# Attention over pooled slots and a top-128 MLP on one core: a planner's start order, GpSimd's drain and the final flag are changed

## Chip, core and metric

The kernel runs on one core of a Trainium2 chip. Its metric is the device time of one execution in microseconds (us). TensorE's weight loads (PEld) and matmuls (PE), VectorE (DVE), ScalarE (ACT), GpSimd (POOL) and SyncE (SP) each take their own instructions in the order in which they stand in the program; semaphores order them against each other.

## The reference, cut to what matters

```python
# q, k, v: 8 batches x 8 heads x 576 rows x 64;  phi: 8 x 8 x 576 x 32
a = softmax(phi, axis=2)                       # over the 576 rows
k_m = einsum('bhsm,bhsd->bhmd', a, k)          # 32 pooled keys per head
v_m = einsum('bhsm,bhsd->bhmd', a, v)          # 32 pooled values per head
x = softmax(q @ k_m.T / 8) @ v_m               # put together to 8 x 576 x 512
for b in range(8):
    top = the 128 rows of x[b] with the highest x[b] @ w_gate
    xe = x[b, top]
    out[b] = x[b]
    out[b, top] = xe + sigmoid(xe @ w_gate)[:, None] * (relu(xe @ w1) @ w2)   # 512 -> 1024 -> 512
```

## The kernel before

**The planner.** The program is written by Python generators (jobs), each of which issues a few instructions and then yields. `in_order_of_time` goes on with the job whose next step is due first by the costs of the class `Plan` (`plan.free` has the time at which each engine is free by these costs). These costs run when the program is built; on the chip only the order that came out of them is left. So a number in the planner moves instructions in all five queues, and changes none of them.

**Softmax of phi.** `softmax(b, chain)` makes an exact exponential of the 128 x 1152 tile of a batch: about twenty VectorE operations over 1152 elements (L381 to L448), half as many on ScalarE between them, and then normalises it (L454 to L476). Two chains take the even and the odd batches. `phi_loader` loads a batch's tile `ph` (L291).

**Keys.** `keys` transposes the finished softmax of a batch on TensorE (L580, four groups of three), splits it into two parts (`ahi` on ScalarE, `alo` on VectorE, L599), stores both to the DRAM tensor `aparts` (L605), and multiplies it with k (L622) to the pooled keys.

**Split of v.** `split_v` takes v in 32 pieces, four a batch, loads one (`vb`, L531, three buffers), rounds it on ScalarE (`vhi`, L548, two buffers), subtracts on VectorE (L550) and stores both parts to the DRAM tensor `vparts` from GpSimd's queue (L554). A piece isn't taken up before 8.0 + 6.5 us times its number by the planner's clock.

**Values.** The pooled values are summed in 116 chunks of 12 columns. Four batches can be under way, each in its 32 rows of the array and its own PSUM bank; `FIRST = [0, 8, 14, 20, 48, 56, 62, 68]` is the chunk with which a batch begins, and it lasts for 48. For every chunk `a_loader` reads `aparts` (L662), `v_loader` reads `vparts` (L686), `widener` spreads the weights over 128 columns in four operations on VectorE (L709) or ScalarE (L711), whichever the planner thinks is free, and `values` multiplies (L731).

**Attention and MLP.** When the pooled values of a batch are there, `centre` centres keys and values on VectorE (its last operation writes `vz`, L797) and TensorE transposes them (L801, L806); then come scores (L835), denominators (L896), products (L910), the gate's scores, the rank of each row (L1001) and the pick of 128 of them. `forward` gathers the picked rows (L1076), multiplies by w1 (L1112) and w2 (L1130), adds (`ye`, L1136) and scatters the rows to the output from GpSimd's queue (L1141). There are eight such scatters.

**The end.** A matmul with `ones` (L1183) sums the marks `good`, two small VectorE operations make the flag `any_bad` (L1185, L1189), every engine loads it into a register (L1190), and a branch (L1191) leaves out a slower general path when the flag is 0. Behind it the program ends with a barrier of all engines in which GpSimd drains (L1228).

## Time and profile before

| | us |
|---|---|
| median of 3 runs | 705.27 |
| lowest and highest | 701.38, 707.96 |
| profiled execution, its own time | 700.01 |
| its span, from the first to the last instruction | 698.3 |

The profiled execution lies below the lowest of the three runs, and its span leaves out 1.71 us of its time. The busy share of an engine says which engine could be the limit of a stage; idle time counts only where something is due that waits for it. The rows themselves stand in the section on rows below.

### The profile page before, as it was taken

How to read it: one execution, taken by the hardware profiler on the slowest of the kernel's cores; microseconds unless marked ns; L12 is line 12 of the kernel's file. 1: busy time of each engine (PE TensorE's matmuls, PEld its weight loads, DVE VectorE, ACT ScalarE, POOL GpSimd, SP SyncE). 2: the span in 40 equal slices, each digit the busy share in tenths (PEclk: the TensorE clock that was granted, in tenths of full speed). 3: DMA queues.
4: the chain of work that ended last, by engine and by line, in shares of the span. 5: the costliest groups of instructions: out<-in, count | busy, mean ns of one | idle time of the engine just before them, and what ended most of it. 6: DMA issues, size and time to landing. Idle time of an engine off the chain costs nothing. (4 is left out here: it accounts for less than half of the span.)

```text
span 698.3 us, 18467 instructions
## 1 busy us (share of the span) xinstructions
PE 469.8 (67%) x7130; PEld 386.9 (55%) x7130; DVE 550.3 (79%) x969; ACT 411.7 (59%) x739; POOL 298.8 (43%) x539
## 2 busy tenths in 40 slices
PE   0003285182651465767589879998999999999980
PEld 0002274172641454656567759878787788666750
DVE  4999999999799889897999969696245897978000
ACT  3457695687767798788665565646344655243110
POOL 6022651545525364674545445556455642112110
PEclk9999555555555789998999889999999999999995
DMA  8046775797958998789999766876648443212000
GB/s 215 3 138 194 247 216 174 227 292 254 285 190 263 316 292 241 228 269 255 329 315 340 227 210 212 261 234 209 186 145 231 131 149 127 76 54 69 31 15 20
DMA packets 69583, 137.37 MB, mean 197 GB/s; under 512 B 14832, under 2 KB 44528, under 8 KB 69488
## 3 DMA queue, kind: packets, MB, share of 16 engines
q0 software_dynamic: 25664, 84.45, 36.7%
q1 hardware_dynamic: 43824, 51.67, 26.6%
q8 instruction: 58, 0.95, 0.6%
q14 instruction: 37, 0.30, 0.2%
HBM read 96.21 MB, written 39.85 MB: 195 GB/s over the span
## 5 line engine op out<-in xcount | busy, mean ns | idle before, releaser
L731 PE MATMUL acc<-v_rows,a_rows 32*128 32x256 f32 x4608 | 223.9, 310 | 89.1 <-ACT a_rows L711 72.2
L731 PEld LDWEIGHTS acc<-v_rows,a_rows 32*128 32x128 f32 x4608 | 205.8, 213 | 112.3 <-ACT a_rows L711 70.9
L711 ACT ACTIVATE a_rows<-a_flat,block_of 128x384 fp32r<-128x384 f32 x306 | 164.8, 604 | 86.9 <-PE acc L731 39.9
L686 POOL DMA_DIRECT2D v_rows<-vparts x232 | 131.3, 579 | 114.4 <-PE acc L731 96.7
L709 DVE TENSOR_SCALAR a_rows<-a_flat,block_of 128x384 fp32r<-128x384 f32 x158 | 59.4, 417 | 51.2 <-PE acc L731 29.2
L662 POOL DMA_DIRECT2D a_flat<-aparts x116 | 65.2, 563 | 59.5 <-ACT a_rows L711 33.1
L580 PE MATMUL bank<-ident,ph 128*96 128x128 f32 x96 | 21.8, 373 | 77.2 <-DVE ph L476 77.2
L580 PEld LDWEIGHTS bank<-ident,ph 128*96 128x96 f32 x96 | 14.7, 192 | 82.2 <-issue 61.5
L554 POOL DMA_DIRECT2D vparts<-vb x32 | 19.5, 610 | 77.9 <-DVE vb L550 75.8
L1112 PE MATMUL bank<-xeT,w 128*128 128x128 f32 x352 | 44.3, 280 | 5.3 <-ACT xeT L1096 5.3
L1112 PEld LDWEIGHTS bank<-xeT,w 128*128 128x128 f32 x352 | 41.0, 192 | 7.8 <-ACT xeT L1096 6.5
L954 POOL DMA_DIRECT2D out<-xj x24 | 16.4, 682 | 56.5 <-DVE xj L950 23.3
L1001 DVE SCALAR_TENSOR_TENSOR marks<-row,tg,wide 128x576 bf16<-128x576 f32 x40 | 32.7, 818 | 8.5 <-ACT row L985 6.8
L997 ACT ACTIVATE marks<-row,tg 128x576 bf16<-128x576 f32 x40 | 31.1, 777 | 1.8
L1130 PE MATMUL bank<-w,hT 128*128 128x512 f32 x64 | 30.3, 607 | 0.0
L548 ACT ACTIVATE vhi<-vb 128x576 fp32r<-128x576 f32 x32 | 21.5, 673 | 14.0 <-DMA vparts<-vhi 8.6
L1130 PE MATMUL acc<-w,hT 128*128 128x512 f32 x64 | 29.0, 599 | 0.0
L963 DVE TENSOR_REDUCE four<-prod 128x128 f32<-128x512 f32 x40 | 27.2, 681 | 0.7
L960 DVE TENSOR_TENSOR prod<-xj,wg 128x512 f32<-128x512 f32 x40 | 27.4, 686 | 0.3
L473 DVE SCALAR_TENSOR_TENSOR ph<-rh,sm,ph 128x576 f32<-128x576 f16 x32 | 26.0, 812 | 1.3 <-ACT rh L462 1.2
L910 PE MATMUL bank<-vbd,eT 64*128 64x128 f32 x272 | 26.6, 297 | 0.0
L1141 POOL DMA_INDIRECT out<-ye,idx x8 | 9.3, 1163 | 40.6 <-DVE ye L1136 25.1
(172 smaller groups left out, 982.9 us busy)
## 6 DMA issues: line engine op xcount, KB each, us to landing
v_rows<-vparts POOLq DMA_DIRECT2D x152, 192.0 KB, 4.3
a_flat<-aparts SPq DMA_DIRECT2D x228, 48.0 KB
vb<-in_v SPq DMA_DIRECT2D x32, 288.0 KB
kb<-in_k SPq DMA_DIRECT2D x32, 288.0 KB
vparts<-vb POOLq DMA_DIRECT2D x32, 288.0 KB, 4.3
vparts<-vhi POOLq DMA_DIRECT2D x32, 288.0 KB, 6.2
qb<-in_qT SPq DMA_DIRECT2D x16, 576.0 KB
out<-xj POOLq DMA_DIRECT2D x16, 512.0 KB, 3.7
```

The costliest lines, as they stand in the source:

```text
L580: nc.tensor.transpose(out=bk([PT, 3, P])[:, c], in_=a[:, c0 + c], identity=ident)
L662: (nc.sync if 2 * t + g < 3 else nc.gpsimd).dma_start(out=a_flat[ch % NF][32 * r0 + 2 * t + g:32 * r1:4] .rearrange("p s m -> p (s m)"), i ...
L686: nc.gpsimd.dma_start(out=v_rows[ch % NV].bitcast(F32)[32 * r0 + g:32 * r1:2, g] .rearrange("p s d -> p (s d)"), in_=src.unsqueeze(1).to_b ...
L709: nc.vector.tensor_scalar_mul(ar[:, :, j], src, block_of[:, j:j + 1])
L711: nc.scalar.activation(ar[:, :, j], src, AF.Copy, scale=block_of[:, j:j + 1])
L731: nc.tensor.matmul(out=accs[b % SET][:, :2 * P].rearrange("p (r g d) -> p r g d", g=NG, d=Dh), lhsT=ar[p, s].rearrange("p j m -> p (j m)") ...
L960: nc.vector.tensor_mul(prod, x[:, c], wg)
L963: nc.vector.tensor_reduce(four, prod.rearrange("p (n f) -> p n f", f=4), axis=AX.X, op=ALU.add)
L997: nc.scalar.activation(sign, row, AF.Sign, bias=g, scale=-1.0, accum_out=less[:, c:c + 1])
L1001: nc.vector.scalar_tensor_tensor(out=cmp, in0=row, scalar=g, in1=wide[:, off:off + S], op0=ALU.is_equal, op1=ALU.mult, accum_out=equal[:, ...
L1112: nc.tensor.matmul(out=bk([P, 4, P])[:, f, :n], lhsT=w1_sb[d][:, (f0 + f) * P:(f0 + f + 1) * P], rhs=xeT[:, d, :n], start=(d == 0), stop=( ...
L1130: nc.tensor.matmul(out=ps[:n], lhsT=hT[:, f, :n], rhs=w2_sb[f], start=(f == 0), stop=(f == KF - 1))
```

## The change

It has seven parts. Five work through the planner alone:

- GpSimd counts as busy until 12 us, when its constants are being written, so that the costs put the first stores behind them;
- a piece of v may be taken up every 5.0 us instead of every 6.5 us;
- the small reduction `block_of` goes from the head of the program to just ahead of the first chunk's load;
- `widener` takes VectorE only when ScalarE is behind by over 600 instead of 100 ns; weights are loaded 5 us apart instead of 4; `keys` has a bias of 0.5 instead of 1 us;
- `forward` loses the head start of 12 us that it had while the planner held TensorE's clock for slow.

Two touch instructions themselves: a drain is issued on GpSimd behind the seventh of the eight scatters, and the sum that makes the flag becomes a job of its own (`checks`), which is due 3 us after the last batch has been ranked, ahead of the last MLPs; the register loads and the branch stay at the end.

```diff
-                x[0] - 12 * 1e3 if not plan.warm.get(plan.at) else max(x[0], free))
+                max(x[0], free))
...
+        plan.free["pool"] = 12 * 1e3
+        plan.begin(0.0)
         nc.sync.dma_start(out=wg, in_=bass.AP(
...
-            yield max(stored[-2], (8.0 + 6.5 * len(done)) * 1e3)
+            yield max(stored[-2], (8.0 + 5.0 * len(done)) * 1e3)
...
     def a_loader():
-        nc.vector.tensor_reduce(block_of, each.rearrange("p b j -> p j b"), axis=AX.X, op=ALU.add)
         for ch in range(COLS // T):
...
             yield written[b]
+            if not ch:
+                nc.vector.tensor_reduce(block_of, each.rearrange("p b j -> p j b"), axis=AX.X,
+                                        op=ALU.add)
+                plan.begin(written[b])
...
-                if plan.free["dve"] + 100 < plan.free["act"]:
+                if plan.free["dve"] + 600 < plan.free["act"]:
...
                 in_=ye[:n], in_offset=None)
+            if i == count - 2 and not general:
+                tc.nc.gpsimd.drain()
             yield e
...
-            yield plan.t + 4e3
+            yield plan.t + 5e3
...
+    any_bad = work.tile([1, 1], I32, name="any_bad")
+
+    def checks():
+        while len(attended) < B:
+            yield lambda: len(attended) == B
+        yield plan.t + 3e3
+        bk = yield from take()
+        ps = bk([1, B])
+        nc.tensor.matmul(out=ps, lhsT=ones, rhs=good, start=True, stop=True)
+        yield
+        bad = work.tile([1, B], I32, name="bad")
+        nc.vector.tensor_scalar(out=bad, in0=ps, scalar1=-1.0, scalar2=float(P * NT * H),
+                                op0=ALU.mult, op1=ALU.add)
+        bk.give()
+        yield
+        nc.vector.tensor_reduce(any_bad, bad, axis=AX.X, op=ALU.max)
...
-        (1 * 1e3, keys()), (0.0 * 1e3, split_v()),
+        (0.5 * 1e3, keys()), (0.0 * 1e3, split_v()),
...
-        (None and None * 1e3, forward(B * nt)), (0.0, load_weights())])
+        (None and None * 1e3, forward(B * nt)), (0.0, load_weights()), (0.0, checks())])
```

The line numbers of the changed kernel are higher than those of the kernel before: by 2 from the loads and softmax on, by 5 from the values on. **At the head of VectorE's queue** there stands before (L381 begins the softmax of the first batch, `block_of` is the small reduction):

```order
L648 TENSOR_REDUCE block_of<-each 128x4
L381 TENSOR_REDUCE mx<-ph 128x2
L384 TENSOR_SCALAR ph<-ph,mx 128x576 x2
L390 SCALAR_TENSOR_TENSOR ph<-q,ph 128x1152
L392 SCALAR_TENSOR_TENSOR ph<-q,ph 128x1152
L400 SCALAR_TENSOR_TENSOR rl<-rh,ph 128x1152
L403 SCALAR_TENSOR_TENSOR num<-num,ph 128x1152
L409 SCALAR_TENSOR_TENSOR den<-den,ph 128x1152
```

VectorE's queue now begins so (L383 is L381 of before, L392 is L390, L552 subtracts a piece of v):

```order
L383 TENSOR_REDUCE mx<-ph 128x2
L386 TENSOR_SCALAR ph<-ph,mx 128x576 x2
L383 TENSOR_REDUCE mx<-ph 128x2
L392 SCALAR_TENSOR_TENSOR ph<-q,ph 128x1152
L386 TENSOR_SCALAR ph<-ph,mx 128x576 x2
L394 SCALAR_TENSOR_TENSOR ph<-q,ph 128x1152
L392 SCALAR_TENSOR_TENSOR ph<-q,ph 128x1152
L552 TENSOR_TENSOR vb<-vb,vhi 128x576
L394 SCALAR_TENSOR_TENSOR ph<-q,ph 128x1152
```

The reduction into `block_of` has left the head of the queue, and the second batch's softmax and the first piece of v stand between the steps of the first batch.

**On TensorE, around the first scores** (the first L835), there stands before, behind the end of the value chunk that is the 55th, the transpose of batch 0's centred values (L801, L806):

```order
L731 MATMUL acc_78<-v_rows_109,a_rows_112 128x256
L731 MATMUL acc_75<-v_rows_109,a_rows_112 128x256
L801 MATMUL bank_81<-ident,vz 128x128
L806 MATMUL bank_79<-ident,vsum 128x128 x4
L835 MATMUL bank_82<-qb,kT_91 32x288
L835 MATMUL bank_80<-qb,kT_91 32x288
```

Now TensorE's queue has at the same place, behind the 58th chunk (L582 is L580 of before, here the third of four groups of batch 6's softmax):

```order
L736 MATMUL acc_75<-v_rows_109,a_rows_113 128x256
L736 MATMUL acc_76<-v_rows_109,a_rows_113 128x256
L806 MATMUL bank_81<-ident,vz 128x128
L811 MATMUL bank_82<-ident,vsum 128x128 x4
L582 MATMUL bank_79<-ident,ph 96x128 x3
L840 MATMUL bank_81<-qb,kT_91 32x288
L840 MATMUL bank_80<-qb,kT_91 32x288
```

The first scores now stand behind three more chunks and behind a transpose that reads the softmax of batch 6; before, all of that softmax, its keys (L622) and their transpose were ahead of the 54th chunk.

**At the end of VectorE's queue**, up to the branch, there stands before:

```order
L1136 SCALAR_TENSOR_TENSOR ye<-bank_80,gr,xe 128x512
L1136 SCALAR_TENSOR_TENSOR ye<-acc_77,gr,xe 128x512
L1185 TENSOR_SCALAR bad<-bank_79 1x8
L1189 TENSOR_REDUCE any_bad<-bad 1x1
L1190 TENSOR_LOAD any_bad
```

And now (L1191 and L1195 are L1185 and L1189 of before, L1141 is the addition `ye`):

```order
L1191 TENSOR_SCALAR bad<-bank_80 1x8
L1195 TENSOR_REDUCE any_bad<-bad 1x1
L1141 SCALAR_TENSOR_TENSOR ye<-acc_78,gr,xe 128x512
L1141 SCALAR_TENSOR_TENSOR ye<-bank_80,gr,xe 128x512
L1205 TENSOR_LOAD any_bad
```

The flag is made ahead of the last two additions. Drains aren't listed in these orders; on GpSimd the new one stands between the seventh and the eighth scatter, with nothing else between these two.

## Rows read from the trace of the kernel before

**Rows 1.** Stretches: busy PE, PEld, DVE, ACT, POOL (instructions); clock, DMA share, GB/s.

```profile
0.00:366.00 366.00, 175.19 (x3142) 153.32 (x3142) 335.72 (x436) 263.33 (x404) 169.79 (x317) 0.75 0.77 235
366.00:440.00 74.00, 64.59 (x1175) 55.23 (x1175) 65.76 (x168) 41.45 (x95) 36.76 (x66) 0.88 0.79 250
440.00:679.00 239.00, 230.00 (x2818) 178.38 (x2815) 148.23 (x365) 106.91 (x240) 91.25 (x156) 1.00 0.44 136
```

**Rows 2.** The same view of stretches of the first 40 us.

```profile
0.00:5.00 5.00, 0.00 (x0) 0.00 (x0) 0.00 (x0) 1.28 (x1) 4.32 (x18) 1.00 0.55 150
5.00:10.00 5.00, 0.00 (x0) 0.00 (x0) 2.71 (x4) 0.00 (x0) 4.79 (x10) 1.00 1.01 263
0.00:20.00 20.00, 0.00 (x0) 0.00 (x0) 10.18 (x10) 7.92 (x7) 10.79 (x39) 1.00 0.76 190
20.00:40.00 20.00, 0.00 (x0) 0.00 (x0) 19.41 (x15) 7.97 (x8) 0.00 (x0) 1.00 0.00 0
```

**Rows 3.** Waits of VectorE, 0 to 100 us: total us, times, longest.

```profile
DVE block_of L648 <- POOL each L329: 7.3, 1, 7.3
DVE rl L400 <- ACT rh L394: 1.2, 1, 1.2
DVE ph L390 <- ACT q L388: 1.2, 1, 1.2
```

**Rows 4.** Line L384 by itself: ns minimum, median, maximum; first and last start.

```profile
L384 DVE TENSOR_SCALAR ph<-ph,mx x16: 507/512/1347, 8.7 to 293.8; 128x576 f32<-128x576 f32 x16
```

**Rows 5.** Groups of VectorE's instructions: busy us, mean ns of one.

```profile
L709 DVE TENSOR_SCALAR a_rows<-a_flat,block_of 128x384 fp32r<-128x384 f32 x158 | 59.4, 417 | 51.2 <-PE acc L731 29.2 <-DMA a_flat<-aparts 8.4 <-issue 7.3
...
L550 DVE TENSOR_TENSOR vb<-vb,vhi 128x576 f32<-128x576 f32 x32 | 23.9, 748 | 0.9 <-ACT vhi L548 0.8
...
L411 DVE SCALAR_TENSOR_TENSOR num<-rl,num 128x1152 f32<-128x1152 f32 x16 | 21.6, 1349 | 0.1
...
L599 DVE TENSOR_TENSOR alo<-aS,ahi 96x768 f32<-96x768 f32 x16 | 14.8, 944 | 0.0
```

**Rows 6.** VectorE in order of time at 348 us: start, duration.

```profile
348.26 0.28 DVE L797 TENSOR_TENSOR vz<-v_m,vsum 128x128 f32<-128x128 f32 x1
```

**Rows 7.** TensorE in order of time, 318 to 372 us.

```profile
330.76 1.70 PE L731 MATMUL acc<-v_rows,a_rows 32*128 32x256 f32 x48
...
339.93 1.55 PE L622 MATMUL bank<-kb,aS 96*32 96x64 f32 x96
...
349.29 0.71 PE L835 MATMUL bank<-qb,kT 64*32 64x288 f32 x16
...
361.14 0.58 PE L580 MATMUL bank<-ident,ph 128*96 128x128 f32 x3
```

**Rows 8.** Line L1228 by itself, the end of the program (q marks an engine's sequencer).

```profile
L1228 POOLq DRAIN  x3: 46/108/10036, 687.4 to 698.0; - x3
L1228 SPq DRAIN  x3: 7/7/13, 688.1 to 697.7; - x3
```

**Rows 9.** Line L1218 by itself, the start of the program.

```profile
L1218 POOLq DRAIN  x1: 194/194/194, 0.4 to 0.4; - x1
```

**Rows 10.** Line L1191 by itself, the branch and what follows it.

```profile
L1191 PEldq COMPARE_BRANCH  x1: 4232/4232/4232, 680.3 to 680.3; - x1
...
L1191 POOLq INC_SWDGE_SEM  x1: 2622/2622/2622, 684.8 to 684.8; - x1
```

**Rows 11.** The eight scatters (L1141): us from issue to landing.

```profile
DMA to landing us min/median/max: 2.8/2.9/5.2
```

**Rows 12.** GpSimd in order of time from 660 us, its last two scatters.

```profile
664.30 0.99 POOL L1141 DMA_INDIRECT out<-ye,idx  x1 [12.34 <-DVE ye L1136]
679.69 0.96 POOL L1141 DMA_INDIRECT out<-ye,idx  x1 [14.41 <-DVE any_bad L1189]
```

**Rows 13.** Line L548 by itself: ScalarE's waits ahead of it, total us, times.

```profile
  DMA vparts<-vhi: 8.6, 4
```

**Rows 14.** Waits of TensorE, 200 to 440 us: total us, times, longest.

```profile
PE acc L731 <- DMA v_rows<-vparts: 9.7, 6, 2.2
```

More of the change, by code (lines that the diff above doesn't have):

```diff
@@ L1170, in load_weights @@
                 w2_sb.append(t[:, x])
-            yield plan.t + 4e3
+            yield plan.t + 5e3
+    any_bad = work.tile([1, 1], I32, name="any_bad")
[13 more added lines that the diff above has]
+        nc.vector.tensor_reduce(any_bad, bad, axis=AX.X, op=ALU.max)
     late_consts()
@@ L1175 @@
         (lambda: ahead(0), chain([[0, 2, 4, 6], [1, 3, 5, 7]][0], 0)), (lambda: ahead(1), chain([[0, 2, 4, 6], [1, 3, 5, 7]][1], 1)),
-        (1 * 1e3, keys()), (0.0 * 1e3, split_v()),
+        (0.5 * 1e3, keys()), (0.0 * 1e3, split_v()),
         (0.0, phi_loader()), (0.0, k_loader()), (0.0, q_loader()), (0.0, a_loader()), (0.0, v_loader()), (0.0, widener()),
         (0.0 * 1e3, values()), (0.0 * 1e3, attentions(0)), (0.0 * 1e3, attentions(1)),
-        (None and None * 1e3, forward(B * nt)), (0.0, load_weights())])
-    bk = first_free()
-    ps = bk([1, B])
-    nc.tensor.matmul(out=ps, lhsT=ones, rhs=good, start=True, stop=True)
-    bad = work.tile([1, B], I32, name="bad")
-    nc.vector.tensor_scalar(out=bad, in0=ps, scalar1=-1.0, scalar2=float(P * NT * H),
-                            op0=ALU.mult, op1=ALU.add)
-    bk.give()
-    any_bad = work.tile([1, 1], I32, name="any_bad")
-    nc.vector.tensor_reduce(any_bad, bad, axis=AX.X, op=ALU.max)
+        (None and None * 1e3, forward(B * nt)), (0.0, load_weights()), (0.0, checks())])
     taken = nc.values_load(any_bad[0:1, 0:1])
```

## The prediction, made before the changed kernel was timed

> **What bounds the kernel now.** I read the busy time by stretches first, since the bound changes on the way [rows 1]. Up to 366 us, when the last softmax of phi is done, VectorE is busy for 335.7 of 366 us and TensorE for 175.2: VectorE sets the pace. From 366 to 440 us both are nearly full (65.8 and 64.6 of 74). From 440 to 679 us TensorE is busy for 230.0 of 239 us at a granted clock of 1.00, its higher level: it is the bound, and what it has done by then counts, not when any one step was ready. Then comes a tail in which nothing computes. So a gain has three places: VectorE's idle time early, the work that TensorE has already behind it when it becomes the bound, and the tail.
>
> Early, the reader is to see three things. VectorE is idle for 20.0 - 10.2 = 9.8 of the first 20 us and for only 0.6 of the next 20, in which the DMA engines stand still (share 0.00) [rows 2]. The idle time has three names: 7.3 us behind GpSimd's constants (through the small reduction, which waits for them at the head of the queue) and twice 1.2 us for ScalarE, with one chain alone at work [rows 3].
>
> Of the tail the waits and the sequencers' rows tell. The last scatter is issued at 679.69 us [rows 12]. GpSimd's sequencer then spends 2.62 us from 684.8 us on its DMA semaphores [rows 10], and 10.04 us from 687.4 us in a drain, to 697.4; the span ends 0.9 us later, at 698.3 [rows 8].
>
> **The drain.** All sums go against the profiled span of 698.3 us. Is the drain's time a cost of what was issued before it, or of the place? GpSimd's drain at the start of the program took 194 ns [rows 9], and the two that follow the long one 108 and 46 ns [rows 8]; only the one with 680 us of GpSimd's work and DMAs behind it was long. I take it for a cost of that work, so a drain behind the seventh scatter pays it there. That scatter's issue ends at 664.30 + 0.99 = 665.3 us and the eighth starts at 679.69 us [rows 12]: 14.4 us in which GpSimd has nothing else, while TensorE runs the last MLP. The 10.0 us fit, with 4.4 to spare; a drain of over 14.4 us would delay the last scatter by the difference. At the end a short drain is left, of 0.05 to 0.2 us by the other rows. Next late is SyncE, whose own drains begin at 688.1 us [rows 8], 0.7 us into the long one. So the barrier comes at about 688.2 instead of 697.4 us: **-9.2 us**, with 0 as the other end, if the cost belongs to the place.
>
> The Trainium skill speaks against this: its page VectorE: DVE Perf Modes, section The DRAIN you can't avoid, says of the drains around a kernel that they are constant, about 12 ns, on all five engines. This trace agrees for SyncE (7 to 13 ns) and disagrees for GpSimd (10,036 ns), and the measurement decides. By that rule a drain would have no backlog to pay ahead, and the sum would lose its 9.2 us; that is the third rival below, priced there from rows.
>
> **The flag.** It was ready last, so every engine loaded it at 679.7 us; TensorE's branch took 4.23 us from 680.3, to 684.5 [rows 10]. Now TensorE can branch about 1 us earlier. But the last scatter's landing takes up to 5.2 us from its issue [rows 11], to 684.9, and the semaphore step at 684.8 us waits for that as well; the scatter itself waits for the addition, not for the flag. So the flag gives **0**, at most 1 us. Its own instructions (0.2 us of TensorE, 0.3 of VectorE) move under the last MLPs.
>
> **The start.** VectorE no longer waits for the constants but for the first tile of phi. Each batch is 590 kB; in the first 5 us 150 GB/s x 5 = 750 kB were moved, and 1,315 kB in the next 5 [rows 2]. The first tile, alone at the head of SyncE's queue, has thus landed at about 4.5 us. The second comes behind 590 + 262 (the gate's weights) kB, so 1,442 kB must have moved: at 7.6 us if nothing else shared the engines, at some 12 us if all that is issued by then does; I take 10. Since the second batch's first step now stands ahead of L390 (the order at the head of the queue), VectorE does 1.34 + 2 x 0.9 us by 7.7 us and then waits for 2.3 us. Idle becomes 4.5 + 2.3 = 6.8 instead of 9.8 us; the two waits for ScalarE go, since there are two chains to take turns. L384 took 1,347 ns once, beside GpSimd's constants, and 512 ns in the median [rows 4]; now both batches' pairs run there, which I put at 0.8 us. **VectorE gains 9.8 - 6.8 - 0.8 = 2.2 us** (0 to 5, by the two bounds of the landing).
>
> **The order of the softmaxes.** The rest of VectorE's early order only permutes work on a full engine, so I count what stands ahead of a gate in its queue, by durations of the groups [rows 5]. Ahead of the end of batch 0's softmax there are now 12 more operations of 1.35 us and 8 more splits of v of 0.75, with small ones +21 us; ahead of batch 1's end -22, batch 3's -11 x 1.35 + 3 x 0.75 = -12.6, batch 6's +22, batch 7's -5. Two batches now end close together where they followed one another. That changes when chunks can run, but the first scores need all of it: before, they stood behind `vz`, which ended at 348.26 + 0.28 = 348.5 us [rows 6]; now they stand behind the third transpose of batch 6's softmax. Ahead of `vz` before and of that softmax's last step now stands the same work but for 3 more operations of 1.35, two `alo` (0.94) and two widenings (0.42) fewer: +1.3 us. So this gate falls at 348.5 + 1.3 - 2.2 = 347.6, and with the transpose of 0.58 us the scores start at about 348.3 instead of 349.29 us [rows 7]: 1.0 us.
>
> What TensorE has done by then is the larger part. Ahead of the first scores there are now three more chunks, 3 x 1.70 = 5.1 us, but not yet batch 6's keys (1.55) and its last three transposes (0.58) [rows 7]; two transposes of 0.33 cancel. That is 3.0 us of work ahead. From there TensorE has the same work as before, and if it idles as much as before (9.4 + 9.0 us [rows 1]), the end comes **1.0 + 3.0 = 4.0 us** earlier. Below this lie stalls of the early splits, above it waits that vanish; both are rivals. The widenings moved to ScalarE take 23 x 0.42 us from VectorE, most of it after 366 us, where VectorE has 8 us to spare; ScalarE has more. I put them, the weights' spacing and the MLP's lost head start at 0, within those two ends: the same matmuls change places on a full engine.
>
> **The sum.** 698.3 - 9.2 - 4.0 = 685.1 us of span, 686.8 with the 1.71 us outside it. The profiled execution lies 5.3 us under the median of the runs, which I take for their scatter, so I take the difference from the median: 705.27 - 13.2 = **692.0 us**.
>
> **The rivals.**
>
> *Loads stop being late.* The early splits move v's traffic into 20 to 40 us, where DMA stood still, and take it from the crowded stretch in which TensorE waited for `v_rows` six times, 9.7 us in all [rows 14]. If all that goes: 692.0 - 9.7 = 682.3 us. For it speaks a DMA share of 0.77 to 366 us that includes an empty 20 us; against it, that VectorE, not DMA, is full there.
>
> *The change doesn't do what it says at the start.* VectorE was busy for 19.41 of the 20 us in which the earlier loads were to help [rows 2], so an earlier softmax of batch 1 is only a later one of batch 0, and the lead of 4.0 us is used up in waits. Only the drain is left: 705.27 - 9.2 = 696.1 us.
>
> *The drain costs its time at the place.* The 10 us come again at the end: 705.27 - 4.0 = 701.3 us. For it speaks that the semaphore step just ahead of the drain is long too; against it the 194 ns at the start.
>
> *The splits hold up the softmaxes, and it is slower.* 13 splits now stand ahead of batch 0's end instead of 5, and a split waits for a buffer whose store must land: ScalarE waited so four times, 8.6 us in all, 2.15 each [rows 13]. In order, VectorE and both chains wait behind it, and through batch 6's softmax the scores. At 2.15 us each: 692.0 + 13 x 2.15 = 720 us; from 13.2 / 13 = 1.0 us each on, the kernel is slower than before. Against it: one to four operations of 1.35 us stand between a split and the next, and DMA was empty there.
>
> **How the numbers follow.** Forecast 0.40, loads no longer late 0.20, drain alone 0.17, drain at the place 0.15, splits in the way 0.08. Runs of this kernel differ by some 6 us, so about 1% (7 us: 698.2 and 712.3) is what a measurement tells from no change. Faster by more: nearly all of the forecast (0.36), the loads (0.20), most of the drain alone (0.13) and a little of the drain at the place (0.02), 0.71. Slower by more: 0.08. Within: 0.21. The range goes from the loads' case (682.3) to the drain at the place with some of the runs' scatter (701.3 + 2), 682 to 703 us; left out are the slow rival and the lower half of the first.
>
> **What would show it.** A GpSimd drain of about 10 us inside the stretch of the last MLP, and one under 0.3 us at the end; the span ending 9 to 10 us after the last scatter instead of 18.6. VectorE's first step at 4 to 5 us and its first scores' gate at 346 to 349. TensorE 58 chunks in at the first scores. The prediction is wrong if the last drain is still long, if the rows of L548 show waits of over 1 us ahead of most early splits, or if TensorE idles for much more or less than 18 us from 366 to 679 us.

## The result, and the profile after

| | before | after |
|---|---|---|
| median of 4 runs, us | 703.47 | 683.30 |
| lowest, highest | 701.38, 707.96 | 678.99, 691.14 |
| median without the slow run | 703.47 | 681.03 |
| profiled execution, its own time | 700.01 | 681.03 |
| its span | 698.3 | 679.2 |

Here and below, a run that lies over 1.5% above the fastest of its kernel (here the one of 691.14 us) counts as slow and is left out of the medians and ratios that are compared. The kernel became faster: after/before is 0.9685, 95% interval 0.9596 to 0.9773. The medians so taken differ by 22.4 us and the profiled executions by 19.0, where 13.2 were forecast. The forecast time of 692.0 us is 11.0 too high, and 681.0 us lies 1.0 under the end of the forecast range; with three runs, from 679.0 to 685.6 us, it is known to some 6 us only.

The tail comes first. In the kernel after, L1151 is the new drain, L1206 the branch with the step INC_SWDGE_SEM behind it (the semaphore step), L1243 the end of the program. Each line is seen by itself: ns minimum, median, maximum, then first and last start in us.

```profile
L1151 POOLq DRAIN  x1: 11192/11192/11192, 658.5 to 658.5; - x1
...
L1206 PEldq COMPARE_BRANCH  x1: 3712/3712/3712, 667.5 to 667.5; - x1
...
L1206 POOLq INC_SWDGE_SEM  x1: 195/195/195, 677.4 to 677.4; - x1
...
L1243 POOLq DRAIN  x3: 46/108/139, 677.7 to 678.9; - x3
L1243 SPq DRAIN  x3: 7/7/13, 678.3 to 678.6; - x3
```

The last two scatters, in order of time:

```profile
658.76 0.99 POOL L1146 DMA_INDIRECT out<-ye,idx  x1 [10.63 <-DVE ye L1141]
674.16 0.98 POOL L1146 DMA_INDIRECT out<-ye,idx  x1 [14.41 <-DVE ye L1141]
```

Against [rows 8, 10 to 12]: the last scatter is issued 5.5 us earlier, and from there to the end it takes 5.0 us in place of 18.6. The long drain now lies behind the seventh scatter, ends at 658.5 + 11.2 = 669.7 us and is over 4.5 us before the eighth. The end has a drain of 0.14. Two things shrank that I had left at nothing: the semaphore step is 195 ns in place of 2622, and it begins 3.2 us after the last scatter instead of 5.1.

Of the front, the first stretches and the stages (columns as in [rows 1]), VectorE's waits from 0 to 100 us, and VectorE in order of time:

```profile
0.00:20.00 20.00, 0.00 (x0) 0.00 (x0) 14.19 (x14) 10.04 (x10) 12.44 (x41) 1.00 0.53 176
20.00:40.00 20.00, 0.00 (x0) 0.00 (x0) 20.00 (x19) 16.25 (x17) 4.42 (x8) 1.00 0.62 204
...
0.00:366.00 366.00, 184.78 (x3333) 163.27 (x3333) 337.69 (x448) 268.78 (x417) 171.53 (x322) 0.79 0.77 236
366.00:440.00 74.00, 62.65 (x1107) 51.50 (x1111) 61.64 (x150) 45.50 (x105) 38.26 (x70) 0.91 0.85 270
```

```profile
DVE mx L383 <- DMA ph<-in_phiT: 5.8, 2, 4.6
```

```profile
4.61 1.35 DVE L383 TENSOR_REDUCE mx<-ph 128x2 f32<-128x1152 f32 x1 [4.61 <-DMA ph<-in_phiT]
5.99 1.43 DVE L386 TENSOR_SCALAR ph<-ph,mx 128x576 f32<-128x576 f32 x2
8.59 1.35 DVE L383 TENSOR_REDUCE mx<-ph 128x2 f32<-128x1152 f32 x1 [1.17 <-DMA ph<-in_phiT]
```

VectorE begins at 4.6 us, waits only for phi, and has 4.0 us more done by 20 us than before [rows 2, 3]. The first scores:

```profile
346.04 1.72 PE L840 MATMUL bank<-qb,kT 64*32 64x288 f32 x16 [2.81 <-ACT vbd L817]
347.69 4.00 PE L736 MATMUL acc<-v_rows,a_rows 32*128 32x256 f32 x96
```

They start at 346.0 us (349.3 before [rows 7]), behind 58 chunks, counted from the matmuls of L736. But they did not wait for what was forecast. VectorE's last step for the third transpose of batch 6, ScalarE just ahead of the first scores, the transpose, and VectorE up to its gate before and now:

```profile
341.12 0.81 DVE L478 SCALAR_TENSOR_TENSOR ph<-ph,sm,rh 128x576 f32<-128x576 f32 x1
```

```profile
342.86 2.13 ACT L716 ACTIVATE a_rows<-a_flat,block_of 128x384 fp32r<-128x384 f32 x4 [0.55 <-DMA a_flat<-aparts]
344.90 1.09 ACT L817 ACTIVATE vbd<-bank 32x128 f32<-32x128 f32 x4
```

```profile
342.73 0.49 PE L582 MATMUL bank<-ident,ph 128*96 128x128 f32 x3
```

```profile
0.00:348.54 348.54, 160.45 (x2900) 141.71 (x2900) 318.98 (x401) 252.05 (x379) 162.53 (x303) 0.74 0.76 231
```

```profile
0.00:341.93 341.93, 165.35 (x2942) 147.76 (x2942) 318.84 (x400) 255.95 (x387) 163.94 (x308) 0.78 0.76 232
```

VectorE was through with this step at 341.9 us and TensorE with the transpose at 343.2. The scores then waited 2.8 us for ScalarE: the first of them is written to the bank into which the centred values were transposed (`bank_81` in TensorE's order), and ScalarE copied these out into `vbd` only behind four widenings.

### The profile page after: what moved, and what is told of

It is laid out like the page before. It is cut to its first block, busy times and chain, and to the rows that moved or that the text cites. A ratio compares the mean times of both kernels' runs of the same rounds, so it can differ in the third digit from the quotient of the medians.

```text
span 679.2 us, 18437 instructions
## 1 busy us (share of the span) xinstructions
PE 471.8 (69%) x7130; PEld 388.7 (57%) x7130; DVE 541.7 (80%) x946; ACT 421.3 (62%) x762; POOL 296.7 (44%) x539
## 4 chain that ended last, share of the span: by engine, by line
PE 43%; DMA 19%; DVE 15%; issue 10%; ACT 7%; POOL 4%; SPq 2%; POOLq 0%; DVEq 0%; ACTq 0%
PE acc L736 17%; DMA a_flat<-aparts 8%; PE bank L1117 5%; PE acc L1135 4%; ACT a_rows L716 4%; PE bank L1135 3%; PE acc L1117 3%; DMA aparts<-ahi 3%; PE bank L915 2%; DMA v_rows<-vparts 2%; PE bank L901 2%; PE bank L840 2%; POOL v_rows L691 1%; DMA qb<-in_qT 1%; DMA vparts<-vb 1%
## 5 line engine op out<-in xcount | busy, mean ns | idle before, releaser
L736 PE MATMUL acc<-v_rows,a_rows 32*128 32x256 f32 x4608 | 225.8, 313 | 56.7 <-ACT a_rows L716 33.1
L736 PEld LDWEIGHTS acc<-v_rows,a_rows 32*128 32x128 f32 x4608 | 207.9, 215 | 77.5 <-ACT a_rows L716 38.4
L716 ACT ACTIVATE a_rows<-a_flat,block_of 128x384 fp32r<-128x384 f32 x329 | 175.9, 604 | 85.9 <-PE acc L736 32.9
L714 DVE TENSOR_SCALAR a_rows<-a_flat,block_of 128x384 fp32r<-128x384 f32 x135 | 51.3, 421 | 43.3 <-PE acc L736 15.8
L667 POOL DMA_DIRECT2D a_flat<-aparts x116 | 64.6, 558 | 46.0 <-ACT a_rows L716 14.4
L582 PE MATMUL bank<-ident,ph 128*96 128x128 f32 x96 | 20.2, 361 | 90.3 <-DVE ph L478 89.9
L582 PEld LDWEIGHTS bank<-ident,ph 128*96 128x96 f32 x96 | 15.5, 192 | 93.8 <-issue 76.2
L1117 PE MATMUL bank<-xeT,w 128*128 128x128 f32 x320 | 41.6, 281 | 1.6 <-ACT xeT L1101 1.4
L1117 PEld LDWEIGHTS bank<-xeT,w 128*128 128x128 f32 x320 | 37.6, 192 | 4.8 <-ACT xeT L1101 1.8
L1135 PE MATMUL acc<-w,hT 128*128 128x512 f32 x80 | 37.6, 603 | 0.0
L1006 DVE SCALAR_TENSOR_TENSOR marks<-row,tg,wide 128x576 bf16<-128x576 f32 x40 | 32.7, 818 | 5.6 <-ACT row L990 4.0
L550 ACT ACTIVATE vhi<-vb 128x576 fp32r<-128x576 f32 x32 | 21.5, 673 | 17.1 <-DMA vparts<-vhi 16.4
L624 PE MATMUL bank<-kb,aS 96*32 96x64 f32 x768 | 20.3, 271 | 12.3 <-DMA kb<-in_k 10.5
L1146 POOL DMA_INDIRECT out<-ye,idx x8 | 8.2, 1021 | 44.3 <-DVE ye L1141 31.1
L552 DVE TENSOR_TENSOR vb<-vb,vhi 128x576 f32<-128x576 f32 x32 | 24.1, 752 | 3.1 <-ACT vhi L550 3.1
```

The lines of the kernel that those rows point to most:

```text
L582: nc.tensor.transpose(out=bk([PT, 3, P])[:, c], in_=a[:, c0 + c], identity=ident)
L667: (nc.sync if 2 * t + g < 3 else nc.gpsimd).dma_start(out=a_flat[ch % NF][32 * r0 + 2 * t + g:32 * r1:4] .rearrange("p s m -> p (s m)"), i ...
L714: nc.vector.tensor_scalar_mul(ar[:, :, j], src, block_of[:, j:j + 1])
L716: nc.scalar.activation(ar[:, :, j], src, AF.Copy, scale=block_of[:, j:j + 1])
L736: nc.tensor.matmul(out=accs[b % SET][:, :2 * P].rearrange("p (r g d) -> p r g d", g=NG, d=Dh), lhsT=ar[p, s].rearrange("p j m -> p (j m)") ...
L1006: nc.vector.scalar_tensor_tensor(out=cmp, in0=row, scalar=g, in1=wide[:, off:off + S], op0=ALU.is_equal, op1=ALU.mult, accum_out=equal[:, ...
```

## The experiments

I call *tail* the drain and the flag, *front* all the rest, and *the start* three edits of the front: GpSimd's counted time, the place of `block_of`, the keys' 0.5. Each ratio (this/before) is to the kernel before, run on the same chip; its medians there were 701.6 to 702.6 us.

### The tail in parts

The drain alone and the flag alone in the kernel before; both there; the kernel after without the drain. The drain's edit is the same two lines wherever it is added:

```diff
+            if i == count - 2 and not general:
+                tc.nc.gpsimd.drain()
```

The flag's edit is the job `checks` of the change in place of the lines behind the planner.

> The kernel before with the drain behind the seventh scatter and nothing else. Theory: the drain alone takes both long steps out of GpSimd's end: its last drain falls from 10.04 us to about 0.14 and the step that counts its DMAs up (INC_SWDGE_SEM) from 2.62 us to about 0.20, while the last scatter's landing stays near 4.8 us, since the flag is still made late. From the last scatter to the end 18.6 - 9.9 - 2.4 = 6.3 us, and the whole 12.3 us shorter than the kernel before (about 688 beside 700). Rival A, the step INC_SWDGE_SEM was shortened by the early flag: 8.7 us from the last scatter to the end, whole 9.9 shorter. Rival B, the landing was shortened by the drain: landing about 3.0 us, 4.5 us to the end, whole 14.1 shorter. Rival C, the drain holds up the last block: the last scatter is issued later than 679.7 by some us of its 11.

> The kernel before with the flag made early (beside the attentions) and nothing else. Theory: the last scatter lands in about 3.0 us in place of 4.8, because the branches fetch their code before it; GpSimd's last drain stays near 10 us and INC_SWDGE_SEM near 2.6 us; 16.8 us from the last scatter to the end in place of 18.6, whole 1.8 shorter. Rival A, the flag does nothing: 18.6 us, whole unchanged within 1. Rival B, INC_SWDGE_SEM falls to 0.2 with the flag: 14.4 us to the end, or 16.2 with the landing at 4.8.

> The kernel after without the drain. Theory: GpSimd's last drain is back at about 10 to 11 us and INC_SWDGE_SEM at 2.6; 5.0 + 9.9 + 2.4 = 17.3 us from the last scatter to the end, whole 12.3 longer than the kernel after (about 693 beside 681). Rival, the drain cost its 11 us partly at its place, where the last block waits: the last scatter is issued earlier than 674.2 by what it cost there, and the whole is less than 12.3 longer.

> The kernel before with drain and early flag, without the front. Theory: the tail as in the kernel after, 5.0 us from the last scatter to the end, the last scatter where it was in the kernel before (679.7): whole 13.6 shorter than the kernel before (about 686.5 beside 700), and the front is worth the 5.5 us that are left to the kernel after. Rival, the front is worth its predicted 4.0 us and no more: about 685. Rival, the front is worth nothing, the kernel after's earlier last scatter being the spread of runs: about 681.

| | median, us | this/before (95%) | last scatter | from it to the semaphore step | to the end |
|---|---|---|---|---|---|
| before | 702.6 | | 679.7 | 5.1 | 18.6 |
| drain alone | 689.1 | 0.9802 (0.9768 to 0.9836) | 680.7 | 4.9 | 6.7 |
| flag alone | 701.0 | 0.9976 (0.9938 to 1.0015) | 681.2 | 3.6 | 17.2 |
| both | 689.9 | 0.9827 (0.9791 to 0.9862) | 678.2 | 3.3 | 5.1 |
| after without drain | 696.2 | 0.9915 (0.9876 to 0.9953) | 678.6 | 3.6 | 17.2 |

The last three columns are of the profiled executions. The sequencers' rows of the drain alone, and then of the flag alone:

```profile
L1146 POOLq DRAIN  x1: 11188/11188/11188, 665.1 to 665.1; - x1
...
L1193 POOLq INC_SWDGE_SEM  x1: 195/195/195, 685.6 to 685.6; - x1
...
L1230 POOLq DRAIN  x3: 46/108/139, 685.9 to 687.1; - x3
```

```profile
L1200 PEldq COMPARE_BRANCH  x1: 3912/3912/3912, 674.5 to 674.5; - x1
...
L1200 POOLq INC_SWDGE_SEM  x1: 2622/2622/2622, 684.8 to 684.8; - x1
...
L1237 POOLq DRAIN  x3: 46/108/10036, 687.5 to 698.1; - x3
```

For the tail the theory held in all four: the drain takes 9.9 us out of the last drain and 2.4 out of the semaphore step; the flag takes 1.5 out of the time ahead of that step, since TensorE's branch (3.9 us) now ends before the scatter is issued. They add up: 11.9 + 1.4 = 13.3, and 13.5 together. The drain shows no price at its place: from the start of the seventh scatter to that of the eighth it takes 15.4 us before ([rows 12]) and 15.4 in the kernel after, and 15.4 to 15.5 in the profiles of all kernels with the one drain or none. The time of the last scatter itself can't show it, since it moves between executions of one order of work: with the drain it is issued 1.0 us later in one pair of profiles (679.7 and 680.7) and 3.0 and 4.4 earlier in the two others. In part for the same reason the kernel after without the drain is 15.2 us slower than with it, where 12.3 were expected. The flag's 1.4 us is seen in the rows alone; the timed runs can't tell it from 0.

### What a drain's time depends on

One more drain behind the first scatter, at 471 us; then drains behind the first, third, fifth and seventh.

```diff
-            if i == count - 2 and not general:
+            if i in (0, count - 2) and not general:
```

```diff
-            if i == count - 2 and not general:
+            if i in (0, 2, 4, count - 2) and not general:
```

> The kernel after with one more drain, behind the first scatter (472 us). Theory, a drain takes a time in proportion to the DMAs that GpSimd issued since the last one: 11.19 x 373/482 = 8.7 us behind the first scatter and 11.19 x 109/482 = 2.5 us behind the seventh, 0.14 at the end. Rival A, the first long drain of a program has one price: 11.2 us and then about 0.1. Rival B, each drain inside the program costs the same: 11.2 and 11.2. The loads of values and of a that GpSimd issues behind the first scatter wait for it, three v_rows tiles stand ready, so TensorE is idle some 4 to 7 us more between 472 and 490, and the whole is as much longer (about 686 beside 681); a drain that costs nothing at such a place would leave it at 681.

> The kernel after with drains behind the first, third, fifth and seventh scatter. With two drains, behind the first and the seventh, the first took 3.8 us and the second 10.3. Theory: a drain is the landing of the scatter ahead of it (3 us) and some 67 ns for each DMA that stands in a ring not yet cleared: 3.8 us behind the first scatter, 3 + 92 x 0.067 = 9.2 us behind the third, then 13 DMAs and 3.9 us, then 4 or 5 DMAs and 3.3 us. Rival A: the price hangs on the gathers and scatters since the last drain (4, 4 and 4 of them here): about 5.4 us each of the last three. Rival B: it is the last one, behind the seventh scatter, that is long wherever the others stand: 3.8, 3.8, 3.8 and 10.

The drains one by one, of two and then of four:

```profile
L1151 POOLq DRAIN  x1: 3825/3825/3825, 470.4 to 470.4; - x1
...
L1151 POOLq DRAIN  x1: 10285/10285/10285, 661.3 to 661.3; - x1
```

```profile
L1151 POOLq DRAIN  x1: 4281/4281/4281, 470.7 to 470.7; - x1
...
L1151 POOLq DRAIN  x1: 8885/8885/8885, 569.1 to 569.1; - x1
...
L1151 POOLq DRAIN  x1: 3587/3587/3587, 635.2 to 635.2; - x1
...
L1151 POOLq DRAIN  x1: 3242/3242/3242, 668.6 to 668.6; - x1
```

With two, all three theories fell: the first drain, with 373 DMAs issued by then, was the short one (3.8 us for 8.7). The next theory was 3 us for the scatter's landing and (10,285 - 3,000)/109 = 67 ns for each of the 109 DMAs since the last drain, and it was put to four drains: 9.2, 3.9 and 3.3 us expected behind the third, fifth and seventh scatter, 8.9, 3.6 and 3.2 measured. Both rivals fell. What stays inferred: the single drain's 11.2 us is the price of (11.2 - 3)/0.067 = 122 DMAs and the first scatter's of 12 to 19, so something must have cleared what was issued before about the 360th; no row shows that.

Two drains: 684.1 us, 0.9758 (0.9711 to 0.9806). The timed runs do not tell this from the kernel after. But the stretch in which the added drain stands, from chunk 72 to the end of chunk 115, took 153.9 us, against 150.2 in the kernel without any drain and 149.5 in the kernel after (its row is further down). That is the size expected, but 1.5 to 2 us of it are idle time and the rest busy time, at a mean granted clock of 0.98 for 1.00; with one execution of each a price of the first drain is likely, not shown:

```profile
424.00:577.90 153.90, 146.90 (x2315) 119.11 (x2316) 102.76 (x265) 88.18 (x194) 81.80 (x144) 0.98 0.61 185
```

```profile
429.40:579.60 150.20, 144.69 (x2317) 116.91 (x2316) 102.82 (x265) 87.98 (x194) 81.64 (x144) 1.00 0.61 190
```

Four: 691.3 us, one run. There the drain behind the third scatter stands ahead of the loads of the last chunks:

```profile
569.35 1.05 POOL L1146 DMA_INDIRECT out<-ye,idx  x1 [0.52 <-DVE vsum L798]
578.62 1.13 POOL L691 DMA_DIRECT2D v_rows<-vparts  x2 [8.22 <-issue]
```

```profile
PE acc L736 <- DMA v_rows<-vparts: 4.7, 1, 4.7
```

GpSimd stands for 8.2 us and TensorE then waits 4.7 for `v_rows`, in one go. Of the places tried, a drain cost nothing at the one where GpSimd had nothing else to issue.

### The front: the start, and the head start

The first kernel has the start and the tail, with these edits against the kernel after:

```diff
-                max(x[0], free))
+                x[0] - 12 * 1e3 if not plan.warm.get(plan.at) else max(x[0], free))
...
-            yield max(stored[-2], (8.0 + 5.0 * len(done)) * 1e3)
+            yield max(stored[-2], (8.0 + 6.5 * len(done)) * 1e3)
...
-                if plan.free["dve"] + 600 < plan.free["act"]:
+                if plan.free["dve"] + 100 < plan.free["act"]:
...
-            yield plan.t + 5e3
+            yield plan.t + 4e3
```

The second is the kernel after with the start undone (and the weights 4 us apart, as above):

```diff
-        plan.free["pool"] = 12 * 1e3
-        plan.begin(0.0)
...
-            if not ch:
-                nc.vector.tensor_reduce(block_of, each.rearrange("p b j -> p j b"), axis=AX.X,
-                                        op=ALU.add)
-                plan.begin(written[b])
...
+        nc.vector.tensor_reduce(block_of, each.rearrange("p b j -> p j b"), axis=AX.X, op=ALU.add)
-        (0.5 * 1e3, keys()), (0.0 * 1e3, split_v()),
+        (1 * 1e3, keys()), (0.0 * 1e3, split_v()),
```

The third is the kernel after with forward's head start back (the first edit of the first piece) and keys at 1.0.

> Drain, early flag and, of the front, only the three edits of the start (GpSimd's counted time behind its fills, the sum that makes block_of moved behind the first written values, keys at 0.5); the splits' pace, forward's head start, the widening rule and the pace of the weights are as in the kernel before. Theory: VectorE's first step ends at 6.0 us and it has about 14.2 us of work done by 20 us, against 10.2 in the kernel before, and these 4.0 us reach the end: about 4 shorter than the kernel with drain and flag alone, 16.5 shorter than the kernel before. Rival: the start alone is lost again before the last chunk, and the order of the splits and softmaxes carries the front: VectorE starts as early, but the whole is within 1 us of drain and flag alone (12.6 shorter than the kernel before).

> The kernel after with the three edits of the start undone, and the pace of the weights (4 us) with them; the splits' pace 5.0, no head start for forward and the widening rule of 600 stay, with drain and flag. Theory: VectorE has about 10.2 us of work done by 20 us again and the whole is some 4 longer than the kernel after (about 17 shorter than the kernel before). Rival: the rest carries the front: within 1 us of the kernel after (about 21 shorter than the kernel before). Rival: without the start the rest is worth less than nothing, being late splits in front of the first softmaxes: 12 shorter than the kernel before or less.

> The kernel after with forward's head start of 12 us restored (and keys at 1.0 in place of 0.5, without which the order does not come out). Theory: the stage from 440 us on is bound by TensorE's work, and moving MLP work ahead of the last chunks only changes which part comes last: within 1.5 us of the kernel after. Rival A: the lead of 19 us that chunk 58 has over the kernel before and that is 7 at chunk 68 was given up because MLP work no longer fills TensorE's waits before 440 us: whole 3 to 5 shorter. Rival B: the blocks' gathers and scatters, put in front of the loads on GpSimd, hold up v_rows: whole 2 to 4 longer.

The theory of the start fell: alone it lies with the tail alone (690.1 and 689.9 us), though VectorE had its 4 us more done by 20 us (14.4 us of work for 10.2). With the start undone the kernel is 4.8 us shorter than the kernel before, less than the tail alone gives: of its three theories the last one, that the rest of the front without the start is worth less than nothing, came true. The kernel with the head start back is 12.7 us slower than the kernel after. Rival B has the sign (2 to 4 us longer), but not the size, and that run had the keys' number in it too, so I took the two apart: the head start dropped in the kernel with the tail alone and in the one with the start alone, and the keys put back alone.

```diff
-                x[0] - 12 * 1e3 if not plan.warm.get(plan.at) else max(x[0], free))
+                max(x[0], free))
```

```diff
-        (0.5 * 1e3, keys()), (0.0 * 1e3, split_v()),
+        (1 * 1e3, keys()), (0.0 * 1e3, split_v()),
```

> Drain and early flag with the kernel before's front, but forward without its head start of 12 us; nothing else. Theory: forward's first gather is no longer issued just ahead of the MLP's first transposes, so TensorE's wait of 3.3 us for xe goes and some of the 19.0 us that it idles between chunk 48 and chunk 72: 3 shorter than drain and flag alone (about 15.6 shorter than the kernel before). Rival A: without the start's lead there is nothing for it to keep: within 1 of drain and flag alone (12.6 shorter than the kernel before). Rival B: the head start's loss is the whole front: 6 to 7 shorter than drain and flag alone (19 shorter than the kernel before).

> The kernel of the start alone (drain, flag, the start's three edits) with forward's head start dropped as well. Theory: the start brings chunk 48 forward by 3 to 6 us and the head start wastes it between chunk 48 and chunk 72, where TensorE idled 26.3 us in place of 21.5 in the kernel after; without it that is 21 to 22 us again and the whole is 5 to 7 shorter than the start alone (about 18 shorter than the kernel before). Rival: the splits' pace is what counts, and this kernel lies with the start alone, 12 shorter than the kernel before, TensorE idle over 25 us there.

> The kernel after with the keys' starting time at 1.0 in place of 0.5, nothing else: the control for the head start restored, which needed this too and was 10 us longer. Theory: the keys do nothing, within 1.5 us of the kernel after (about 20 shorter than the kernel before), and chunk 48 starts at 314 to 316 us. Rival: the 10 us came from the keys' place: about 12 to 14 shorter than the kernel before, with TensorE idle 28 us between chunk 48 and chunk 72.

Against both theories, dropping the head start *cost* 4 us in the one kernel (the intervals overlap) and 16 in the other, and nothing that can be told with the keys at 1.0 (691.9 dropped, 693.7 kept). Putting the keys back by 0.5 us cost 11.

### A mechanism, or another order?

Four kernels, each the kernel after but for one number: keys at 0.0, at 0.25, the widening rule at 100, the weights 4 us apart.

```diff
-        (0.5 * 1e3, keys()), (0.0 * 1e3, split_v()),
+        (0.25 * 1e3, keys()), (0.0 * 1e3, split_v()),
```

> The kernel after with the keys' starting time at 0.0 in place of 0.5, nothing else. Theory, another draw of the order: above the kernel after, 5 to 20 us (8 to 15 shorter than the kernel before, or less), with TensorE's idle time between chunk 48 and chunk 115 and its granted clock there spread differently. Rival, earlier keys are better: at the kernel after's time or under it (20 or more shorter than the kernel before), the waits for kb under 2.8 us.

> The kernel after with the keys' starting time at 0.25 in place of 0.5, nothing else. Theory, another draw: 5 to 20 us above the kernel after, and not between the times of 0.0 and 0.5 but by its own order. Rival, earlier keys are better: at the kernel after's time within 1.5 us (some 20 shorter than the kernel before).

> The kernel after with the widening rule at 100 in place of 600, nothing else. By the prediction's step these widenings are worth 0: within 1.5 us of the kernel after. Theory, another draw of the order: 5 to 15 us above it. Rival, a mechanism (23 widenings of 0.42 us off VectorE): 2 to 9 us above it, with VectorE's busy time up to 366 us some 3 to 9 us longer.

> The kernel after with the pace of the weights' loads at 4 us in place of 5, nothing else; the order changes only from about matmul row 2600 on, behind the first scores. By the prediction's step it is worth 0: within 1.5 us of the kernel after. Theory, another draw: 2 to 10 us above it, all of it behind chunk 56.

All kernels of this table but the first have the tail. The last four columns are of the profiled execution: when chunk 48 starts, how long TensorE idles and is busy from there to the last scatter (summed over stretches as in the rows below), and when the last scatter is issued; it is the sum of the other three. Busy time is longer where more of the work is left at chunk 48, and where the granted clock is lower.

| | median, us | this/before (95%) | chunk 48 | idle | busy | last scatter |
|---|---|---|---|---|---|---|
| before | 701.6 to 703.5 | | 325.7 | 29.8 | 324.2 | 679.7 |
| tail alone | 689.9 | 0.9827 (0.9791 to 0.9862) | 323.3 | 28.8 | 326.1 | 678.2 |
| after | 681.0 | 0.9685 (0.9596 to 0.9773) | 314.8 | 31.6 | 327.8 | 674.2 |
| start alone | 690.1 | 0.9833 (0.9798 to 0.9867) | 320.0 | 34.4 | 327.6 | 682.0 |
| start undone | 697.5 | 0.9950 (0.9922 to 0.9978) | 330.7 | 30.6 | 325.9 | 687.2 |
| tail alone, no head start | 693.9 | 0.9887 (0.9844 to 0.9931) | 323.7 | 32.7 | 327.5 | 683.9 |
| start alone, no head start | 706.0 | 1.0054 (1.0016 to 1.0091) | 320.1 | 43.2 | 336.4 | 699.7 |
| after, head start, keys 1.0 | 693.7 | 0.9887 (0.9849 to 0.9926) | 314.9 | 38.9 | 330.5 | 684.3 |
| after, keys 1.0 | 691.9 | 0.9850 (0.9810 to 0.9890) | 315.0 | 35.9 | 333.6 | 684.5 |
| after, keys 0.25 | 703.2 | 1.0017 (0.9975 to 1.0059) | 309.5 | 54.6 | 332.8 | 697.0 |
| after, keys 0.0 | 693.9 | 0.9899 (0.9860 to 0.9938) | 308.3 | 44.3 | 334.2 | 686.9 |
| after, widening 100 | 686.8 | 0.9796 (0.9724 to 0.9869) | 308.7 | 40.2 | 332.9 | 681.8 |
| after, weights 4 us | 688.0 | 0.9829 (0.9766 to 0.9893) | 312.3 | 37.5 | 331.0 | 680.8 |

The keys at 0.0, 0.25, 0.5 and 1.0 give 694, 703, 681 and 692 us: no trend, so no mechanism of earlier keys. Widening and weights, undone, lie 5.7 and 6.9 us above the kernel after in the median, but their intervals overlap its own. The rival for the widenings, VectorE 3 to 9 us longer busy up to 366 us, fell (336.5 us, 337.7 in the kernel after).

How much of a column is chance? The kernel after without the drain and the one with two drains have exactly its order of work on every engine: in their profiles chunk 48 starts at 317.2 and 314.6 us, TensorE idles 33.5 and 37.6, and the last scatter is issued at 678.6 and 676.9. So a few us between two rows of these columns need not come from the order.

In the kernel that lost most to the head start (start alone, 690.1 and 706.0 us) half of the loss in the profiles is idle and half busy time, 8.8 us each. Its last stretch, and that of the start alone:

```profile
588.40:699.70 111.30, 99.63 (x631) 73.55 (x627) 51.74 (x120) 28.18 (x65) 15.05 (x18) 0.94 0.14 48
```

```profile
583.20:682.00 98.80, 94.49 (x647) 69.14 (x643) 53.20 (x123) 28.34 (x67) 14.21 (x21) 1.00 0.19 60
```

TensorE waited there for ScalarE's `xeT` for 6.5 us in two goes (1.4 in the start alone), and the mean granted clock was 0.94, so the lower of the two levels for a part of the stretch; in the start alone it was 1.00.

The stretches of the kernel after (to chunk 72, to the end of chunk 115, to the last scatter), and of the kernel with keys at 0.25:

```profile
314.80:425.60 110.80, 89.27 (x1723) 74.58 (x1722) 91.67 (x203) 74.36 (x163) 51.60 (x94) 0.88 0.83 261
425.60:575.10 149.50, 144.43 (x2315) 116.74 (x2316) 103.00 (x265) 87.96 (x194) 81.43 (x144) 1.00 0.62 191
575.10:674.20 99.10, 94.11 (x643) 68.74 (x639) 52.51 (x122) 28.05 (x66) 13.21 (x20) 1.00 0.18 57
```

```profile
309.50:433.90 124.40, 89.79 (x1735) 76.56 (x1734) 104.14 (x215) 81.55 (x173) 51.87 (x94) 0.88 0.81 250
433.90:598.80 164.90, 149.24 (x2324) 121.38 (x2324) 99.17 (x254) 89.56 (x197) 82.08 (x147) 0.97 0.57 175
598.80:696.95 98.15, 93.79 (x627) 68.66 (x623) 51.28 (x119) 27.77 (x65) 12.55 (x17) 1.00 0.15 52
```

And what TensorE waits for in the first of these stretches, in the one and in the other:

```profile
PE acc L736 <- ACT a_rows L716: 4.8, 5, 2.4
...
PE bank L624 <- DMA kb<-in_k: 2.8, 1, 2.8
```

```profile
PE acc L736 <- ACT a_rows L716: 9.0, 5, 3.9
PE bank L624 <- DMA kb<-in_k: 6.9, 1, 6.9
PE bank L582 <- DVE ph L478: 5.1, 2, 2.8
```

The second kernel is 5.3 us ahead at chunk 48 and 8.3 behind at chunk 72. It idles 34.6 instead of 21.5 us between them, behind widenings, keys' loads and a softmax that its order puts too late for where their matmuls stand, and 15.7 instead of 5.1 us up to chunk 115. The prediction priced none of these waits apart from the sum of idle time.

## Why the prediction came out as it did

**The drain.** Right in kind: a cost of what was issued before, paid ahead under the last MLP, with SyncE's steps next late. The step that failed is the size of the term "-9.2 us" (11.9 measured with the drain alone). It took one of GpSimd's two long steps, and left the semaphore step of 2.62 us beside it as a point that "speaks for" the rival of a cost at the place. It was the same cost, and the drain took 2.4 us of it as well. The Trainium skill's page VectorE: DVE Perf Modes, section The DRAIN you can't avoid, says of the drains around a kernel that they are constant, about 12 ns, on all five engines; this case's traces don't agree for GpSimd, whose last long drain took 10,036 ns in the kernel before and 139 in the one after.

**The flag.** The term was put at 0, at most 1 us, and was 1.4 in the rows. I saw that the branch ended at 684.5 us and the landing at 684.9 and took the second for independent of the first; with the branch out of the way the step behind the landing begins 3.3 to 3.6 us after the scatter instead of 4.9 to 5.1. That TensorE's branch as such delays the landing is likely by the order in time and not shown: the early flag moved the branches of several engines at once. What a branch does in its 4 us (the expectation has it fetch code) no run here singles out.

**The tail together**: 13.6 us for 9.2. Of the 11.0 us by which 692.0 misses, 4.4 are here. 1.8 are the basis (a median of 705.27 then, 703.47 with the fourth run), 1.5 the last scatter's (5.5 us earlier for 4.0), and 3.3 remain between medians and single executions: the profiled one of the kernel before lies 3.5 us under its median, that of the kernel after on it.

**The start.** Mechanism right, size low: phi's second tile was there at 8.6 us and not at 10, and VectorE gained 4.0 us by 20 us for 2.2, inside the bounds of 0 to 5.

**The gate of the first scores.** Here a step failed in kind: "this gate falls at 348.5 + 1.3 - 2.2 = 347.6". VectorE's step ended at 341.9 us, with the same 319 us of work ahead of it as the gate of before but 23.1 us of idle time for 29.6. Besides the start, its widenings waited 2.8 us for `a_flat` in place of 8.4, which the prediction didn't price. What the scores waited for last was ScalarE's `vbd`, which it didn't have at all. So 346.0 us lies near the forecast 348.3 by two errors against each other, and the term "1.0" was 3.3. The 58 chunks were as said.

**From there to the end** the prediction rests on two sentences, "if it idles as much as before" and "I put them, the weights' spacing and the MLP's lost head start at 0". For the kernel after the first holds: 31.6 us of idle time from chunk 48 on, 29.8 before. So the last scatter came 5.5 us earlier, near the 4.0, though the lead at the first scores (3.3 us and three chunks' 3.0) was 6.3. But the second is wrong as a statement on the edits. In the orders that these numbers draw, the idle time runs from 28.8 to 54.6 us, and the lost head start costs about 0, 4 or 16 us by what else stands in the program. That one unchanged value for this term came out near was luck of this order, not knowledge.

**The rivals.** The loads did not stop being late, though their 682.3 us lies close to the result: TensorE's wait for `v_rows` from 200 to 440 us grew from 9.7 [rows 14] to 14.2 us. ScalarE's wait for the buffers of the splits grew too, from 8.6 [rows 13] to 16.4 us, without holding up the first scores:

```profile
PE acc L736 <- DMA v_rows<-vparts: 14.2, 7, 4.5
```

```profile
  DMA vparts<-vhi: 16.4, 8
```

"The change doesn't do what it says" is right for the start alone (it ends with the tail alone) and wrong for the whole front. How much the front brings is known only to some us: the medians give 702.6 - 22.4 - 689.9 = -9.7 against the tail alone and 696.2 - 701.0 = -4.8 with the flag and no drain. Why the orders with the keys at 0.0 and 0.25 idle 13 and 23 us more than this one stays open: their waits lie in a different place in each. For the nearer neighbours (4 to 9 us more) even the difference in idle time is not clear, since its own order had 37.6 us with one more drain.

## What to carry to other kernels

GpSimd's long steps at the end of a program are a debt for DMAs that it issued: look for all of them in the sequencer's rows, and pay them with one drain in a stretch where GpSimd has nothing to issue and another engine is the bound; make the final branch's condition before that stretch. Where a planner sets the order, a bias is no mechanism but the draw of another order: half a microsecond or less in one bias cost 11 to 22 us, so keep only what is timed, and put the spread of neighbouring numbers into the range. An early lead is no gain until it is compared with the idle time of the engine that becomes the bound later.

## What was not expected of the hardware

- A drain on GpSimd fits 3.0 us behind a scatter and 67 ns for each DMA that the engine had issued since the last drain (4 to 109 of them, the scatter just ahead not counted), and a part of an older backlog must have gone by itself: 3.8 and 4.3 us with 373 DMAs issued and no drain before, 11.2 with 483. No row shows when it went.
- The end of the program without a drain cost 10,036 + 2,622 ns, the same to the ns in the three kernels without one; behind a drain 139 + 195 ns.
- The final branch took 3.4 to 4.2 us on TensorE's sequencer (45 to 72 ns on the other engines'), and the step behind the last scatter's landing began 1.5 us later when it ran beside it.
